# Moving the output stores of a fused RWKV and gated-SSM kernel from SyncE's queue to ScalarE's

## The chip, the cores and the metric

The kernel runs on one core of a Trainium2 chip. The metric is the device time of one execution in microseconds (us). A time is the median of several runs. A ratio is taken from the fast runs of one kernel and the fast runs of the other in the same rounds, so it is not quite the ratio of the medians quoted beside it. A run over 1.5% above the fastest of its kernel is counted as slow and left out.

Engine names in the profile: PE is TensorE, PEld its weight loads, DVE VectorE, ACT ScalarE, POOL GpSimd, SP SyncE. SPq and ACTq are the sequencers of SyncE and ScalarE, on which DMA issues and their waits stand.

## The reference

Two layers in a row. The first is a linear attention with a decaying state, for 4 x 8 heads, 768 steps and head size 48; the second is a gated state-space layer with a projection in (384 to 2 x 512), a scan, a gate and a projection out (512 to 384).

```python
for t in range(S):                                   # attention
    cur = np.einsum('bhd,bhe->bhde', u[None] * kt, vt)
    y[:, :, t] = np.einsum('bhd,bhde->bhe', rt, state + cur)
    state = wt[:, :, :, None] * state + np.einsum('bhd,bhe->bhde', kt, vt)
...
proj = x @ w_in                                      # gated state space
val, gate = proj[..., :D_inner], proj[..., D_inner:]
for t in range(S):
    h = a[0, 0] * h + val[:, t, :]
    ys[:, t, :] = h
return silu(gate) * ys @ w_out
```

The output is 4 x 768 x 384 float32, 4.72 MB, written as 24 tiles of 128 rows.

## The kernel before

The whole program is a list of words, one per step and piece. Each engine keeps the order of its own words. `ld` is a load, `osb.n` copies the result of output tile n from PSUM to SBUF on ScalarE, and `ship.n` stores it.

```python
ORDER = """
...
K.8:p xT.12 S.15 ld.9.k.0 sc.14 red.8 ...
ld.10.r.0 pv.6.1:1 S.16 scn.6.1 tr.17 K.9:p ship.4 scn.6.2 ln.11 cs.10.P:20 ship.2 sc.16 y.14
...
op.19:1 scn.11.2 op.20:0 osb.19 scn.11.3 op.21:1 ship.19 osb.20 z.11:d op.18:2 ship.20 osb.21
op.22:0 ship.21 osb.18 op.23:1 ship.18 osb.22 ship.22 osb.23 ship.23
"""
# ... cut: tiles; 7 output tiles in a ring, 3 PSUM banks for products, 1 for transposes
osbs = ring("osb", 7, [128, DM], F32)
trp = psum.tile([128, 2, HP, C], BF16, name="trp")
mms = [psum.tile([128, 512], F32, name=f"mm{i}") for i in range(3)]
# ... cut
def trd(n):                      # transpose of a q,k tile by DMA (the last six tiles)
    m, g = divmod(n, G)
    T["QK", n] = t = QKs[n % 3]
    sp.dma_start_transpose(out=..., in_=qk[m % NB][:, g]...)
# ... cut
def osb(n):
    T["osb", n] = osbs[n % 7]
    act.copy(T["osb", n], T["op", n])

def ship(n):
    b, c = divmod(n, CB)
    sp.dma_start(out=out[b, c * C : (c + 1) * C, :], in_=T["osb", n])
```

All transfers are issued by SyncE. Copies fall into three groups: six between 74 and 85 us (tiles 3, 1, 0, 4, 2, 5), twelve between 102 and 133 us, and six at the end.

## Time and profile before

| | before |
|---|---|
| median of 4 runs | 143.55 us (143.32 to 144.97) |
| span of the profiled run | 143.2 us (its device time, 144.88 us, is near the slowest of the four) |
| DMA issues | all on SyncE; 24 stores of 192 KB among them |
| ScalarE in 70 to 80 us | 9.16 of 10 us busy |

The page gives busy time, shares of 40 slices and the chain that ended last; its lines are shown in the prediction below. ScalarE's timeline before (start us, length us, engine, line, operation, output and input, count; in brackets the idle time ahead of it and what ended it):

```profile
74.72 0.85 ACT L100 COPY osb<-mm 128x384 f32<-128x384 f32 x2
75.80 0.48 ACT L100 COPY osb<-mm 128x384 f32<-128x384 f32 x1 [0.23 <-PE mm L100]
76.17 0.48 ACT L100 COPY xT<-trp 128x384 bf16<-128x384 bf16 x1
76.62 0.48 ACT L100 COPY osb<-mm 128x384 f32<-128x384 f32 x1
```

Two copies of 0.48 us take 0.85 us together, because the second starts 0.37 us after the first. ScalarE has almost no gap here.

### The profile page before, as it was taken

The numbers are of one execution on the slowest core, as the hardware profiler recorded it, in microseconds if no ns is written. First come the engines' busy times: TensorE is split into PE (matmuls) and PEld (weight loads), VectorE is DVE, ScalarE is ACT, GpSimd is POOL, SyncE is SP. The second block draws the span as 40 slices with busy tenths as digits, with TensorE's granted clock in tenths as the row PEclk, the third lists the DMA queues.
The fourth block names the chain that finished last, engine by engine and source line by source line (L and its number), as shares of the span: only waits on it lengthen the run. The fifth ranks groups of instructions, "written<-read, shape, count | busy, mean of one in ns | idle before, by whom it ended". The sixth has DMA issues, their size and how long they took to land.

```text
span 143.2 us, 3840 instructions
## 1 busy us (share of the span) xinstructions
PE 116.9 (82%) x1512; PEld 80.6 (56%) x1512; DVE 114.8 (80%) x169; ACT 98.7 (69%) x181; POOL 88.5 (62%) x83
## 2 busy tenths in 40 slices
PE   0288583899577797997799899998999999999990
PEld 0124351477354545876567677865477676767750
DVE  3026899658897679999999999889969989979740
ACT  3294636695767469999897899998587608645461
POOL 7814222195479485944949769983467999295500
PEclk9999999999999879999999999999599999999999
DMA  3999998999999899999999999898999999930435
GB/s 48 236 184 208 213 223 139 232 220 190 232 203 218 189 196 278 173 223 225 267 179 165 202 183 206 170 207 224 182 185 228 179 270 285 240 115 0 165 128 206
DMA packets 101026, 27.98 MB, mean 195 GB/s; under 512 B 95760, under 2 KB 101008, under 8 KB 101008
## 3 DMA queue, kind: packets, MB, share of 16 engines
q1 hardware_dynamic: 101008, 27.73, 95.8%
q8 instruction: 12, 0.20, 0.6%
q14 instruction: 6, 0.05, 0.1%
HBM read 21.43 MB, written 4.72 MB: 183 GB/s over the span
## 4 chain that ended last, share of the span: by engine, by line
PE 23%; SPq 22%; DMA 18%; DVE 16%; ACT 7%; issue 7%; POOL 5%; POOLq 0%; DVEq 0%; ACTq 0%
SPq L100 22%; PE mm L100 14%; DMA QK<-qk 6%; PE yk L100 5%; DVE At L100 4%; DMA stage<-in_moe_w_out_dram 4%; DMA r<-in_r_dram 4%; DMA k<-in_k_dram 3%; DVE hT L100 3%; DVE rk L100 3%; DVE y L100 3%; PE trp L100 2%; POOL dv L100 2%; POOL qk L100 2%; ACT QK L100 2%
## 5 line engine op out<-in xcount | busy, mean ns | idle before, releaser
L100 PE MATMUL mm<-xT,w_in_sb 128*128 128x256 bf16 x288 | 38.9, 279 | 0.8 <-ACT xT L100 0.6
L100 PEld LDWEIGHTS <-w_in_sb 128*128 128x128 bf16 x288 | 26.9, 99 | 6.8 <-issue 2.2
L100 DVE TENSOR_TENSOR At<-att,mask 128x1024 bf16<-128x1024 f32 x24 | 29.1, 1213 | 1.7 <-PE att L100 1.6
L100 POOL TENSOR_TENSOR qk<-r,P 128x768 bf16<-128x768 f32 x10 | 18.2, 1818 | 15.6 <-DVE dv L100 7.6
L100 POOL TENSOR_TENSOR qk<-k,N 128x768 bf16<-128x768 f32 x11 | 20.0, 1818 | 11.0 <-DVE qk L100 4.5
L100 DVE TENSOR_TENSOR_SCAN hT<-a_f,hT,mm 128x256 bf16<-128x256 f32 x32 | 22.4, 734 | 3.2 <-PE mm L100 3.2
L100 PEld LDWEIGHTS <-qk 128*48 128x48 bf16 (+1 forms) x304 | 14.3, 107 | 12.3 <-issue 6.9
L100 ACT COPY QK<-trp 128x1024 bf16<-128x1024 bf16 x18 | 18.3, 1015 | 4.0 <-PE trp L100 3.9
L100 POOL TENSOR_TENSOR rk<-r,u_b 128x768 f32<-128x768 f32 x9 | 16.3, 1815 | 5.1 <-DMA u_b<-in_u_dram 4.9
L100 PE MATMUL mm<-w_out_sb,z 128*128 128x384 bf16 x96 | 19.2, 335 | 0.0
L100 PEld LDWEIGHTS <-QK 48*128 48x128 bf16 x352 | 11.3, 101 | 12.6 <-ACT QK L100 5.9
L100 ACT COPY osb<-mm 128x384 f32<-128x384 f32 x24 | 11.4, 479 | 8.2 <-PE mm L100 7.8
L100 ACT COPY xT<-trp 128x384 bf16<-128x384 bf16 x24 | 11.5, 480 | 7.2 <-PE trp L100 7.0
L100 DVE TENSOR_TENSOR y<-yk,dv 128x384 bf16<-128x384 f32 x24 | 13.1, 547 | 4.0 <-PE yk L100 3.6
L100 ACT ACTIVATE z<-mm 128x512 bf16<-128x512 f32 x24 | 13.8, 598 | 3.2 <-PE mm L100 3.0
L100 ACT ACTIVATE N<-mm 128x384 f32<-128x384 f32 x24 | 10.9, 492 | 7.0 <-PE mm L100 7.0
L100 POOL TENSOR_TENSOR dv<-v,dvec 128x768 f32<-128x768 f32 x9 | 13.3, 1474 | 3.7 <-DVE rk L100 2.8
L100 PE MATMUL trp<-ident,qk 128*128 128x128 bf16 x144 | 13.5, 244 | 2.3 <-POOL qk L100 1.1
L100 PE MATMUL att<-QK 48*128 48x128 bf16 x192 | 11.0, 243 | 4.8 <-ACT QK L100 3.9
L100 ACT ACTIVATE lwp<-w 128x768 bf16<-128x768 f32 (+1 forms) x13 | 10.3, 797 | 6.1 <-DMA w<-in_w_dram 6.0
L100 POOL TENSOR_TENSOR z<-z,hT 128x1024 bf16<-128x1024 bf16 x5 | 10.6, 2125 | 5.6 <-DVE hT L100 3.0
L100 DVE TENSOR_TENSOR rk<-rk,k 128x768 f32<-128x768 f32 x12 | 12.4, 1031 | 0.6 <-POOL rk L100 0.3
(52 smaller groups left out, 175.7 us busy)
## 6 DMA issues: line engine op xcount, KB each, us to landing
k<-in_k_dram SPq DMA_DIRECT2D x24, 192.0 KB, 4.6
r<-in_r_dram SPq DMA_DIRECT2D x24, 192.0 KB, 4.8
v<-in_v_dram SPq DMA_DIRECT2D x24, 192.0 KB, 4.7
out_dram<-osb SPq DMA_DIRECT2D x24, 192.0 KB, 2.4
w<-in_w_dram SPq DMA_DIRECT2D x11, 384.0 KB, 5.4
stage<-in_moe_w_in_dram SPq DMA_DIRECT2D x4, 384.0 KB, 5.0
stage<-in_moe_w_out_dram SPq DMA_DIRECT2D x2, 384.0 KB, 5.7
w<-in_w_dram SPq DMA_DIRECT2D x2, 192.0 KB, 3.4
```

The source lines that it names most:

```text
L100: return lambda *args, **kwargs: self.tc.keep_in_program_order(op(*args, **kwargs))
```

## The change

The intent is that SyncE's queue carries loads alone, and each output tile leaves as soon as it is copied. The words `ship.n` go, and the store is issued on ScalarE's queue right behind the copy.

```diff
-ld.10.r.0 pv.6.1:1 S.16 scn.6.1 tr.17 K.9:p ship.4 scn.6.2 ln.11 cs.10.P:20 ship.2 sc.16 y.14
+ld.10.r.0 pv.6.1:1 S.16 scn.6.1 tr.17 K.9:p scn.6.2 ln.11 cs.10.P:20 sc.16 y.14 adv.16 ex.10.P.0
 ... (cut: the other ship words go likewise)
     def osb(n):
         T["osb", n] = osbs[n % 7]
         act.copy(T["osb", n], T["op", n])
-
-    def ship(n):
         b, c = divmod(n, CB)
-        sp.dma_start(out=out[b, c * C : (c + 1) * C, :], in_=T["osb", n])
+        act.dma_start(out=out[b, c * C : (c + 1) * C, :], in_=T["osb", n])
```

More of the change, by code (lines that the diff above doesn't have):

```diff
@@ L59 @@
 ld.9.v.1 out.15 scn.5.3 sl.5.0 pv.6.0:0 ld.10.r.1 Q.9:p ln.10 y.15 adv.15 scn.6.0 out.14
-ld.10.r.0 pv.6.1:1 S.16 scn.6.1 tr.17 K.9:p ship.4 scn.6.2 ln.11 cs.10.P:20 ship.2 sc.16 y.14
-adv.16 ex.10.P.0 ship.1 scn.6.3 ex.10.P.1 vc.9:p trd.18 At.16 tot.10:1 QK.17 cs.10.N:02 E.10
-z.4:d yT.14 ld.10.k.1 ex.10.N.0 sc.17 tot.11:1 S.17 ru.10:p ex.10.N.1 out.16 At.17 ld.11.r.0
-E.11 cs.11.N:02 xT.14 op.8:1 ex.11.N.0 y.16 ld.10.k.0 adv.18 ex.11.N.1 rk.9 yT.15 sc.18 osb.8
-op.9:0 trd.19 xT.15 z.5:d cs.11.P:21 osb.9 out.17 z.3:d ex.11.P.0 ship.3 pg.7.0:0 At.18 Q.10:p
@@ L65 @@
-ex.11.P.1 ship.0 yT.16 pv.7.0:1 sl.7.0 ld.11.r.1 y.17 op.6:2 scn.7.0 ld.10.v.1 K.10:p out.18
-red.9 sc.19 osb.6 op.7:0 xT.16 ld.10.v.0 S.19 pg.7.1:2 osb.7 At.19 dv.9:p yT.17 ld.11.k.0
-pg.6.1:0 sl.7.1 scn.7.1 xT.17 pg.6.0:2 trd.20 sl.6.1 rk.10 op.10:1 y.18 Q.11:p pv.8.0:0
-ld.11.k.1 osb.10 red.10 sl.6.0 op.11:1 trd.21 scn.8.0 adv.19 osb.11 pg.8.0:2 z.6:p S.20 vc.10:a
-scn.8.1 sc.20 ship.8 pv.7.1:1 sl.8.0 At.20 ld.11.v.1 out.19 adv.20 ship.6 pv.8.1:0 y.19 dv.10:p
-scn.7.2 ship.5 pg.8.1:2 ld.11.v.0 S.21 sc.21 scn.7.3 K.11:p yT.18 adv.21 xT.18 scn.8.2 out.20
@@ L71 @@
-ship.9 sl.8.1 yT.19 ship.10 op.13:1 At.21 xT.19 ship.7 z.7:p op.12:2 osb.13 trd.22 y.20 pv.9.0:1
-osb.12 scn.8.3 out.21 scn.9.0 ship.11 yT.20 pv.9.1:2 vc.11:a ru.11:p y.21 ship.12 pg.9.0:0
-scn.9.1 trd.23 xT.20 S.22 op.15:1 scn.9.2 sl.9.0 sc.22 rk.11 osb.15 yT.21 op.14:0 xT.21 z.8:p
-At.22 pg.9.1:1 osb.14 adv.22 ship.14 sl.9.1 pg.10.0:0 red.11 ship.15 sc.23 scn.9.3 sl.10.0
-out.22 dv.11:p pv.10.1:1 S.23 At.23 op.16:0 z.9:p pg.10.1:2 y.22 osb.16 scn.10.2 out.23 sl.10.1
-yT.22 pv.10.0:0 y.23 xT.22 scn.10.3 yT.23 op.17:2 xT.23 scn.10.0 pv.11.0:1 osb.17 scn.10.1
@@ L77 @@
-ship.17 pg.11.1:2 scn.11.0 z.10:p ship.13 pg.11.0:0 sl.11.1 scn.11.1 ship.16 pv.11.1:2 sl.11.0
-op.19:1 scn.11.2 op.20:0 osb.19 scn.11.3 op.21:1 ship.19 osb.20 z.11:d op.18:2 ship.20 osb.21
-op.22:0 ship.21 osb.18 op.23:1 ship.18 osb.22 ship.22 osb.23 ship.23
+ld.10.r.0 pv.6.1:1 S.16 scn.6.1 tr.17 K.9:p scn.6.2 ln.11 cs.10.P:20 sc.16 y.14 adv.16 ex.10.P.0
+scn.6.3 ex.10.P.1 vc.9:p trd.18 At.16 tot.10:1 QK.17 cs.10.N:02 E.10 z.4:d yT.14 ld.10.k.1
+ex.10.N.0 sc.17 tot.11:1 S.17 ru.10:p ex.10.N.1 out.16 At.17 ld.11.r.0 E.11 cs.11.N:02 xT.14
@@ new lines @@
+op.8:1 ex.11.N.0 y.16 ld.10.k.0 adv.18 ex.11.N.1 rk.9 yT.15 sc.18 osb.8 op.9:0 trd.19 xT.15
+z.5:d cs.11.P:21 osb.9 out.17 z.3:d ex.11.P.0 pg.7.0:0 At.18 Q.10:p ex.11.P.1 yT.16 pv.7.0:1
+sl.7.0 ld.11.r.1 y.17 op.6:2 scn.7.0 ld.10.v.1 K.10:p out.18 red.9 sc.19 osb.6 op.7:0 xT.16
+ld.10.v.0 S.19 pg.7.1:2 osb.7 At.19 dv.9:p yT.17 ld.11.k.0 pg.6.1:0 sl.7.1 scn.7.1 xT.17
+pg.6.0:2 trd.20 sl.6.1 rk.10 op.10:1 y.18 Q.11:p pv.8.0:0 ld.11.k.1 osb.10 red.10 sl.6.0 op.11:1
+trd.21 scn.8.0 adv.19 osb.11 pg.8.0:2 z.6:p S.20 vc.10:a scn.8.1 sc.20 pv.7.1:1 sl.8.0 At.20
@@ new lines @@
+ld.11.v.1 out.19 adv.20 pv.8.1:0 y.19 dv.10:p scn.7.2 pg.8.1:2 ld.11.v.0 S.21 sc.21 scn.7.3
+K.11:p yT.18 adv.21 xT.18 scn.8.2 out.20 sl.8.1 yT.19 op.13:1 At.21 xT.19 z.7:p op.12:2 osb.13
+trd.22 y.20 pv.9.0:1 osb.12 scn.8.3 out.21 scn.9.0 yT.20 pv.9.1:2 vc.11:a ru.11:p y.21 pg.9.0:0
+scn.9.1 trd.23 xT.20 S.22 op.15:1 scn.9.2 sl.9.0 sc.22 rk.11 osb.15 yT.21 op.14:0 xT.21 z.8:p
+At.22 pg.9.1:1 osb.14 adv.22 sl.9.1 pg.10.0:0 red.11 sc.23 scn.9.3 sl.10.0 out.22 dv.11:p
+pv.10.1:1 S.23 At.23 op.16:0 z.9:p pg.10.1:2 y.22 osb.16 scn.10.2 out.23 sl.10.1 yT.22 pv.10.0:0
@@ L80 @@
+y.23 xT.22 scn.10.3 yT.23 op.17:2 xT.23 scn.10.0 pv.11.0:1 osb.17 scn.10.1 pg.11.1:2 scn.11.0
+z.10:p pg.11.0:0 sl.11.1 scn.11.1 pv.11.1:2 sl.11.0 op.19:1 scn.11.2 op.20:0 osb.19 scn.11.3
+op.21:1 osb.20 z.11:d op.18:2 osb.21 op.22:0 osb.18 op.23:1 osb.22 osb.23
 """
@@ L514 @@
         vc=vc, rk=rk, ru=ru, red=red, dv=dv, tr=tr, trd=trd, QK=QK, sc=sc, At=At, adv=adv, S=S, out=out_,
-        y=y, yT=yT, xT=xT, pv=pv, scn=scn, pg=pg, sl=sl, z=z, op=op, osb=osb, ship=ship)
+        y=y, yT=yT, xT=xT, pv=pv, scn=scn, pg=pg, sl=sl, z=z, op=op, osb=osb)
     for word in ORDER.split():
```

## The prediction

> **What bounds the kernel now.** I read the views in this order: the busy table with the slices, the chain of waits, the queue of SyncE (its issues in time and its waits), then ScalarE's timeline around each copy that is to carry a store, and last the table by stretches. The page first, engine busy time in us, then the span in 40 slices of 3.6 us:
>
> ```profile
> PE 116.9 (82%) x1512; PEld 80.6 (56%) x1512; DVE 114.8 (80%) x169; ACT 98.7 (69%) x181; POOL 88.5 (62%) x83
> ...
> ACT  3294636695767469999897899998587608645461
> ...
> DMA  3999998999999899999999999898999999930435
> ...
> PE 23%; SPq 22%; DMA 18%; DVE 16%; ACT 7%; issue 7%; POOL 5%; POOLq 0%; DVEq 0%; ACTq 0%
> ```
>
> No engine is the bound for the whole span. The DMA engines are busy until slice 34 (about 122 us) and then have little to do; ScalarE's 69% hides a stretch, slices 18 to 28 or so, in which it is nearly full. The chain that ended last goes through SyncE's queue and transfers for 40% of the span: up to 32 us it is pure issuing of loads, from 32 to 100 us mostly computing with one transfer in it, and around 100 to 115 us a load and a transposing transfer again, from the chain in order of time (start, length, what):
>
> ```profile
> 100.90 0.43 SPq L100
> 101.33 0.06 issue
> 101.39 0.61 SPq L100
> 102.00 0.05 issue
> 102.05 4.77 DMA k<-in_k_dram
> ```
>
> A second transposing transfer, 4.91 us, stands in the chain at 122.43. After 127.4 us it is computing alone: TensorE to the last product, and a ScalarE copy at 139.60, whose store goes out at 140.1 and lands some 2 us later. What the 24 stores are today, from the list of DMA issues and SyncE's own waits:
>
> ```profile
> out_dram<-osb SPq DMA_DIRECT2D x24, 192.0 KB, 2.4
> ...
> SPq L100 <- ACT osb L100: 12.5, 7, 6.3
> ```
>
> The 12.5 us of waiting for copies are nearly all at the end, after the last load (SyncE has nothing else to do there), so they hold nothing up. The stores that stand between loads are the 13 up to 122.4 us. SyncE's issues there take 3.21 (3 stores, from 96.0), 1.05 (2), 0.52 (1), 1.09 (2), 1.64 (3) and 1.31 us (2): 8.82 us, or 0.68 us each. The first three hold data copied about 20 us before (the first six copies are at 74.7 to 84.7 us, the first store is issued at 96.0).
>
> The stretches, busy us of each engine:
>
> ```profile
> 70.00:80.00 10.00, 9.54 (x147) 6.50 (x147) 9.40 (x13) 9.16 (x20) 6.71 (x6) 1.00 0.94 173
> 80.00:90.00 10.00, 9.60 (x131) 7.43 (x131) 9.69 (x15) 8.95 (x15) 8.56 (x6) 1.00 1.17 197
> ...
> 110.00:120.00 10.00, 9.80 (x135) 6.94 (x133) 9.05 (x14) 5.22 (x11) 8.73 (x6) 1.00 1.09 224
> ```
>
> The columns are PE, PEld, DVE, ACT, POOL, then clock, DMA share and GB/s. From 70 to 90 us PE, DVE and ACT are all at 9 of 10: whatever takes time from one has little slack to hide in. From 110 on ACT has half its time free.
>
> **What the Trainium skill says.** "Perfetto Trace Analysis", section DMA Instruction — HWDGE: the semaphore wait of such an instruction sits on the issuing sequencer, and the descriptor generator is locked for it, being shared by the two sequencers that issue; the sequencer is free only when the descriptors are made. So a store on ScalarE's queue keeps ScalarE from its next instruction until the copy has ended and the issue is done. The trace of before agrees for SyncE (its issues run one after another, its waits are its own), and has no issue on ScalarE, so the lock isn't shown. "DMA: Bandwidth & Descriptors", section Issuing engines are not separate DMA queues: issues from several engines run on the same 16 DMA engines, and a second issuer saves only the sequencer's issue time. The DMA row at 9 until 122 us says that this time isn't all that SyncE is short of. "Perfetto Trace Analysis", section DMA Optimizations, speaks for the change: separating inputs and outputs between issuers may help. "ScalarE: Activation LUTs", section What ACT_TABLE_LOAD costs, has back-to-back ACTIVATEs overlapping by about 93 ns; here two output copies of 0.478 us took 0.85 us together, an overlap of about 0.11 us, which a store between them takes away.
>
> **The change part by part.** No bytes and no arithmetic change. 24 issues leave SyncE, and 24 go to ScalarE, each directly after its copy.
>
> *Taken from SyncE:* 8.82 us of issuing among the loads. The bytes stay, and the DMA engines are saturated there. In the last stretch nine stores of 192 KB run with a DMA share of about 0.46 at 161 GB/s, so a store needs about 197 KB / (161/0.46 GB/s) = 0.56 us of all engines (an estimate); 13 of them are 7.3 us, and in the changed kernel about as many have gone out before the last load. The sum doesn't fall; only its order changes: six stores move from 96 to 119 us into 75 to 86 us. What is gained is that the load at 102.05 us (4.77 us to landing, median of its kind 4.6) and the transposes (4.32 and 4.91 us) stand behind fewer bytes and reach the queue up to about a us earlier. Of 15 us of such pieces in the chain I take **2.0 us** off.
>
> *Put on ScalarE:* one store costs it the issue, about 0.35 to 0.43 us where rings are empty (shortest SyncE store 0.332, median 0.428 us), 0.68 us where loads are in flight, plus about 0.15 us for the lost overlap and for the wait until the copy's semaphore is seen (an estimate, from the 0.11 us above and the 0.02 to 0.05 us between the last copy's end and its store). So about 0.85 us in the loaded stretch, 0.5 us at the end.
>
> Stretch 74.7 to 85 us: 6 stores x 0.85 = 5.1 us. ScalarE's gaps there are 0.23 + 0.60 + 0.55 + 0.29 = 1.7 us, leaving 3.4 us. Its copies empty the single transpose bank and the three product banks, so TensorE follows; I let 80% pass: **+2.7 us**.
>
> Stretch 102 to 114 us: 6 stores, 5.1 us. ScalarE has gaps of 0.2 to 0.9 us before most of its operations, 3.8 us in sum, then a gap of 3.53 us. But each store delays the copy or activation just after it. I let a quarter pass: **+1.2 us**.
>
> Stretch 120 to 133 us: 6 stores, about 4 us, with ScalarE a third to a half free; **+0.7 us**.
>
> The end: the last six copies start at 136.23 and are 0.67 us apart on average (to 139.60), paced by products of 4 matmuls each. With 0.48 + 0.37 + 0.10 = 0.95 us for copy, issue and restart, ScalarE becomes slower than TensorE: 5 x 0.28 = **+1.4 us**. After the last copy the path (issue, 2 us of landing) is as before.
>
> Sum: 2.7 + 1.2 + 0.7 + 1.4 - 2.0 = +4.0 us, or 143.6 + 4.0 = 147.6 us.
>
> **The rivals.** *The loads run free.* If SyncE's issue time itself bounds the stretch from 96 to 123 us, where its queue has hardly a gap, taking off 8.8 us could advance the last loads and transposes by several us, and two rings per DMA engine might fill each other's gaps. For it: SPq is 22% of the chain. Against: most of that 22% is before 32 us, where there is no store; the issue times of about 1 us for loads against 0.4 us for stores say that the issuing is held by engines that are full; and PE is at 9.7 of 10 in 100 to 120 us anyway. It would give 139 to 142 us. *Everything is hidden.* ScalarE is 69% busy, with 44 us free; if the order absorbs the issues in its gaps and the delay of the middle stretch is taken back while the loads get ahead, only the end's 1.4 us remains, less the relief: 143 to 145 us. Against: the gaps of the 70 to 90 us stretch are too few. *The lock bites.* If a ScalarE issue has to wait for SyncE's running issue (load issues of about 1 us, back to back), each store of the loaded stretches costs 1.5 us or more, 12 of them 18 us instead of 10, and a good part of 8 us comes on top: 152 to 156 us. For it: SyncE's queue has no gaps from 70 to 123 us, and one store took 2.242 us to issue. Against: a store's bytes are large pieces on an otherwise empty ring.
>
> **Range and chances.** I take **147.6 us**, range **143.4 to 153.5**: the lower end is the hidden case, the upper the mild form of the lock. Faster by over 2% is below 140.7 us, only the first rival in full: 0.08. Within 2% (140.7 to 146.5) is the hidden case or a larger relief: 0.32. Slower: 0.60.
>
> **What would show it.** In the changed kernel's profile: 24 ScalarE issues of 0.35 to 0.8 us, longer in 75 to 86 us than at the end; ScalarE gaps of 0.5 to 1 us behind each output copy, put down to its own queue; TensorE and VectorE idle more for transposes and product banks from 75 us on; a ScalarE interval of about 0.95 us between the last six copies instead of 0.67; SyncE without store gaps from 96 us, and the load and transposes near 100 to 115 us landing sooner than 4.3 to 4.8 us. The prediction is wrong if the issues cost ScalarE far more (lock) or if ScalarE's delay doesn't reach TensorE; or if the chain after 96 us turns out to have been set by SyncE's queue, so that everything behind it moves up by several us.

## The result, and the profile after

The changed kernel takes 149.43 us (149.14 to 150.57, 4 runs) against 143.55 us, a ratio of 1.0403, 95% interval 1.0316 to 1.049. It is slower. Repeated later, on the same chip and in the same rounds as three of the experiments, it was 149.14 us against 145.39 us, ratio 1.0323 (1.0251 to 1.0394). Its profiled span is 147.9 us.

The page of the changed kernel, the same rows as in the prediction (busy share of ScalarE and of the DMA engines in 40 slices of 3.7 us, the chain by engine, the stores):

```profile
ACT  3284536768677579997956679998487527745541
...
DMA  3999998999989999899897999899996997711153
...
PE 36%; DVE 20%; ACT 16%; SPq 10%; issue 6%; DMA 4%; ACTq 4%; POOL 2%; DVEq 0%
...
out_dram<-osb ACTq DMA_DIRECT2D x24, 192.0 KB, 2.9
```

SyncE and DMA together fell from 40% of the chain to 14%. What replaced them is TensorE (23% to 36%) and ScalarE with its queue (7% to 20%). The span still grew by 4.7 us: the chain left the loads, and became longer.

ScalarE's timeline after, from the first output copy:

```profile
74.50 0.47 ACT L98 COPY osb<-mm 128x384 f32<-128x384 f32 x1
75.00 0.37 ACTq L98 DMA_DIRECT2D out_dram<-osb  x1
75.41 0.48 ACT L98 COPY osb<-mm 128x384 f32<-128x384 f32 x1 [0.45 <-ACT osb L98]
75.92 0.34 ACTq L98 DMA_DIRECT2D out_dram<-osb  x1
76.30 0.48 ACT L98 COPY osb<-mm 128x384 f32<-128x384 f32 x1 [0.41 <-ACT osb L98]
76.81 0.79 ACTq L98 DMA_DIRECT2D out_dram<-osb  x1
77.64 0.48 ACT L98 COPY xT<-trp 128x384 bf16<-128x384 bf16 x1 [0.86 <-PE att L98]
78.01 0.48 ACT L98 COPY osb<-mm 128x384 f32<-128x384 f32 x1
```

A store starts 0.03 us after its copy ends, holds the queue for 0.34 us, and the next operation starts about 0.05 us later. The second copy starts 0.91 us after the first instead of 0.37 us: about 0.5 us per store in which ScalarE works on nothing.

To see where the time went, I set the start of each output copy after against its start before:

| copy | 1 | 2 | 3 | 4 | 5 | 6 | 7 | 12 | 18 | 19 | 22 | 24 |
|---|---|---|---|---|---|---|---|---|---|---|---|---|
| later by, us | -0.2 | 0.3 | 0.5 | 1.4 | 2.8 | 3.0 | 3.3 | 3.6 | 2.9 | 2.9 | 4.3 | 4.8 |

So about 3 us are lost between the first and the sixth copy (74 to 88 us), nothing over the next twelve, and another 1.9 us over the last six. Such a table compares two single traces. In the repeat's trace the first copy is already 1.5 us later, with no store behind it yet, and the sixth is 3.1 us later, so only 1.6 us are lost there. Eight of the thirteen other profiles reach their first copy 0.7 to 2.3 us later than that of before, although nothing ahead of it was changed. The growth within a trace is the better guide.

The end before, and then after:

```profile
136.23 1.09 ACT L100 COPY osb<-mm 128x384 f32<-128x384 f32 x2 [1.00 <-PE mm L100]
137.65 1.08 ACT L100 COPY osb<-mm 128x384 f32<-128x384 f32 x2 [0.33 <-PE mm L100]
138.91 0.48 ACT L100 COPY osb<-mm 128x384 f32<-128x384 f32 x1 [0.17 <-PE mm L100]
139.60 0.48 ACT L100 COPY osb<-mm 128x384 f32<-128x384 f32 x1 [0.22 <-PE mm L100]
```

```profile
140.05 0.48 ACT L98 COPY osb<-mm 128x384 f32<-128x384 f32 x1 [0.47 <-PE mm L98]
140.56 0.91 ACTq L98 DMA_DIRECT2D out_dram<-osb  x1
...
143.46 0.48 ACT L98 COPY osb<-mm 128x384 f32<-128x384 f32 x1 [0.47 <-ACT osb L98]
143.96 0.34 ACTq L98 DMA_DIRECT2D out_dram<-osb  x1
144.40 0.48 ACT L98 COPY osb<-mm 128x384 f32<-128x384 f32 x1 [0.47 <-ACT osb L98]
```

Before, each of these copies waited for TensorE's product (`<-PE mm`). After, the last ones wait for ScalarE's own store, 0.94 us apart. One issue took 0.91 us, which makes this run's end 0.4 us worse than the repeat's (2.9 to 4.4 us later there).

SyncE's own waits in the changed kernel hold something that I had not foreseen (waited for: us in total, times, longest):

```profile
SPq L98 <- DMA out_dram<-osb: 7.9, 4, 4.2
```

SyncE, which now has only loads and transposes, waits for stores to land (5.7 us in 3 waits in the repeat). The compiled list of instructions says why. The compiler gives the transfers of both queues eight completion counters in turn, and a transfer waits until the one before it on its counter has landed. Two instructions of the changed kernel, one of ScalarE and one of SyncE (numbers ahead are places in each engine's order, tails of names are the compiler's; DMAHW0 to DMAHW7 are the counters):

```
98:96 L98 DMACopy out_dram<-osb_195 128x384 [waits DMAHW6_49,Activation_49]
65 L98 DMACopy r2_127<-in_r_dram 128x8x48 [waits DMAHW6_49]
```

The first is the first store; the second is a load of r with no wait but the one on the same counter. It can't go until that store has landed. The trace agrees: SyncE's issue before it ended at 75.36 us, the store was issued at 75.00 and landed at 79.58, and the load was issued at 79.59 (75.65 in the kernel before).

### The profile page after: what moved, and what is told of

It reads as the page before. It is cut to its first block, busy times and chain, and to the rows that moved or that the text cites. A ratio compares the mean times of both kernels' runs of the same rounds, so it can differ in the third digit from the quotient of the medians.

```text
span 147.9 us, 3827 instructions
## 1 busy us (share of the span) xinstructions
PE 119.0 (80%) x1512; PEld 81.4 (55%) x1512; DVE 114.0 (77%) x169; ACT 98.7 (67%) x181; POOL 88.3 (60%) x83
## 4 chain that ended last, share of the span: by engine, by line
PE 36%; DVE 20%; ACT 16%; SPq 10%; issue 6%; DMA 4%; ACTq 4%; POOL 2%; DVEq 0%
PE mm L98 21%; SPq L98 10%; PE yk L98 7%; DVE hT L98 5%; ACT osb L98 5%; PE trp L98 5%; DMA w<-in_w_dram 4%; DVE At L98 4%; ACTq L98 4%; DVE y L98 3%; ACT QK L98 3%; PE att L98 3%; DVE S L98 2%; DVE z L98 2%; DVE rk L98 2%
## 5 line engine op out<-in xcount | busy, mean ns | idle before, releaser
L98 PE MATMUL mm<-xT,w_in_sb 128*128 128x256 bf16 x288 | 39.7, 281 | 1.4 <-ACT xT L98 0.6
L98 ACT ACTIVATE P<-mm 128x384 f32<-128x384 f32 x24 | 10.8, 494 | 2.2 <-PE mm L98 1.8
```

What stands on the lines that cost most here:

```text
L98: return lambda *args, **kwargs: self.tc.keep_in_program_order(op(*args, **kwargs))
```

## The experiments

Three theories. **A:** ScalarE stands still during each store (copy wait and issue), and this costs where it is nearly full. **B:** the stores, issued early, delay loads: by their bytes (B1), or by the shared counters (B2). **C:** only the end matters. All kernels below start from the kernel before, with `ship(n, on)` able to issue on either queue (`ship.3:a` is ScalarE); all were correct.

| run | median, us | before, us | ratio (95% interval) |
|---|---|---|---|
| act_first6 | 145.92 | 144.04 | 1.0169 (1.0071 to 1.0266) |
| act_mid12 | 146.17 | 144.04 | 1.0162 (1.0057 to 1.0268) |
| act_last6 | 146.61 | 144.04 | 1.0204 (1.012 to 1.0288) |
| hold24 | 148.71 | 144.04 | 1.0337 (1.0226 to 1.0447) |
| act_lag1 | 146.49 | 144.69 | 1.0125 (1.0077 to 1.0174) |
| sp_first6_early | 145.62 | 144.69 | 1.0062 (1.0009 to 1.0115) |
| act_first6_rows16 | 146.87 | 144.69 | 1.0137 (1.0079 to 1.0194) |
| act_last18_lag1 | 146.56 | 144.69 | 1.0002 (0.9941 to 1.0064), two fast runs only |
| after_again | 149.14 | 145.39 | 1.0323 (1.0251 to 1.0394) |
| hold24_again | 148.73 | 145.39 | 1.026 (1.0207 to 1.0314) |
| hold_first6 | 145.96 | 145.39 | 1.0072 (1.004 to 1.0104) |
| act_first6_lag1 | 146.29 | 145.39 | 1.0073 (1.0041 to 1.0105) |

The medians are of all runs, the ratios of the fast ones. In the rounds of the last four rows the limit leaves out 13 of 40 runs of the kernel before, but only 4 of the 53 others. That makes these losses look somewhat larger: over all runs the means are 2.9% apart for after_again, 2.4% for hold24_again, 0.56% for hold_first6 and 0.63% for act_first6_lag1.

### Groups of stores, one at a time

act_first6:

```diff
-... osb.3 yT.9 At.13 osb.1 ld.8.r.1 ...   ship.4 ... ship.2 ... (six ship words later)
+... osb.3 ship.3:a yT.9 At.13 osb.1 ship.1:a ld.8.r.1 ...
```

> The kernel before, with only the first six stores (copies at 74 to 85 us) on ScalarE's queue directly behind their copies; the other 18 on SyncE as before. Theory A (ScalarE is held in a stretch where it is nearly full): +3.0 us, the shift of the copies between the two traces at 85 us, so about 146.5 us. Theory B (the early bytes and the waits that they put on the loads cost the time): also slower, and then the early stores on SyncE's queue must cost the same. Theory C (only the end matters): 143.5 to 144 us.

Measured 1.7% (+1.9 us), the sixth copy 2.9 us later, of which 1.6 us remain at the end. The early loss is real and is not an effect of the other stores, but smaller than the 3.0 us read from the two traces. The chain of this run shows where it lies in its profile (start us, length us, what):

```profile
74.78 0.46 ACT osb L98
75.25 0.02 issue
75.27 4.94 DMA out_dram<-osb
80.21 0.02 issue
80.22 0.37 SPq L98
...
81.54 4.30 DMA v<-in_v_dram
85.83 0.03 ACTq L98
85.86 0.04 issue
85.90 0.47 ACT vb L98
```

Here the chain doesn't run through ScalarE's standing still at all. It goes from the first copy to its store, which takes 4.94 us to land, then to SyncE, which was waiting for that landing, then to a load of v, issued late, and to ScalarE's conversion of v. That is B2. The changed kernel's own chain goes the other way over this stretch, through the copies and their stores on ScalarE, and so do those of its repeat and of act_first6_rows16 below:

```profile
74.51 0.46 ACT osb L98
...
75.00 0.37 ACTq L98
...
75.41 0.49 ACT osb L98
```

So both can be at work, and have to be parted.

act_mid12:

```diff
-... osb.8 op.9:0 ...          ship.8 ... (twelve ship words later)
+... osb.8 ship.8:a op.9:0 ...
```

> The kernel before, with only the middle twelve stores (copies at 102 to 133 us) on ScalarE's queue behind their copies. Theory A: no loss, the shift of the copies between the two traces falls by 0.4 us in this stretch, so 143.0 to 144 us. My prediction's term was +1.9 us less 2.0 us of relief, the same sum. If SyncE's queue were a bound after 96 us: 141 us or less.

A miss: 1.6% slower. Its profiled run was a slow one (147.74 us), so it can't explain what the three fast runs lost. Inside it the copies fall 3.5 us behind (from 0.3 us later at copy 9 to 3.8 us at copies 11 and 12), and the chain there has:

```profile
103.35 6.48 DMA QK<-qk
109.83 0.05 issue
109.88 0.40 PE att L97 x8
```

A transposing transfer on SyncE's queue landed 6.5 us after its issue (3.3 to 4.9 us in the six of before), and TensorE stood for it. Whether it does so in the fast runs isn't shown. In the changed kernel the same transfer landed in 3.8 us and isn't in the chain.

These stores aren't free in the changed kernel either. In four of the five kernels that change the first six stores or copies alone, 0.9 to 2.1 us of the early delay come back between copy 6 and copy 18 (act_first6: from 2.9 to 1.6 us later); in the changed kernel and in its repeat 0.1 us does. Its chain runs through copies and their stores there too (a copy at 111.05 us, its store at 111.56). SyncE also waits 3.4 us for stores to land between 107 and 113 us (1.7 us in the repeat). Which of the two keeps the delay isn't shown; holding ScalarE alone doesn't seem to, since hold24 and its repeat get 1.1 and 1.4 us back over these copies.

act_last6:

```diff
-... osb.19 scn.11.3 op.21:1 ship.19 osb.20 z.11:d op.18:2 ship.20 osb.21 ...
+... osb.19 ship.19:a scn.11.3 op.21:1 osb.20 ship.20:a z.11:d op.18:2 osb.21 ship.21:a ...
```

> The kernel before, with only the last six stores on ScalarE's queue behind their copies. Theory A: copies 0.95 us apart instead of 0.67, +1.4 to +1.9 us, 145 to 145.5 us, and together with the first six nearly all of the loss. Theory B (early bytes): no loss, 143.5 us, since nothing is loaded there.

2.0% slower. In the trace its last copies are 0.95 us apart and the shift grows from -0.4 to 1.0 us, 1.4 us; the timed loss is larger than that. C falls, since the first six lose as well. The three groups add to 5.4%, the changed kernel loses 3.2% to 4.0%: the losses aren't additive, one group's delay hides another's.

### ScalarE held, nothing stored from it

hold24 and hold24_again:

```diff
         act.copy(T["osb", n], T["op", n])
+        act.copy(T["osb", n], T["osb", n])
```

> The kernel before, all stores on SyncE as before, but each output copy is followed by a second copy of the tile onto itself (same values), which keeps ScalarE about 0.5 us longer after its first copy, as a store does, without any change to transfers. Theory A: as slow as the changed kernel, 148 to 151 us. Theory B (the order of transfers is what costs): 143.5 to 145 us.

> The run in which every output copy is done a second time and no store is moved, once more: its first look had a profiled run 1.9 us longer in span than that of before, its timed runs 3.4% more. If standing still is all of the loss, it is as slow as the changed kernel in the same rounds, 4% over before. If the shared counters make a part of 1 to 1.5 us, it is 2.5 to 3.3% over before and the changed kernel about 1% slower than it.

3.4%, and 2.6% in the repeat. All transfers keep their queue and their order, and ScalarE's standing still is replaced by work of about the same length:

```profile
74.59 0.47 ACT L97 COPY osb<-mm 128x384 f32<-128x384 f32 x1
75.10 0.51 ACT L97 COPY osb<-osb 128x384 f32<-128x384 f32 x1
75.52 0.47 ACT L97 COPY osb<-mm 128x384 f32<-128x384 f32 x1
```

Output copies are 0.93 us apart, as in the changed kernel (0.91 us). So holding ScalarE alone makes most of the loss: 2.6 of 3.2 points in the same rounds. A part of the 2.6 is the second copy's own: the last store now waits for it and goes out 0.57 us after the last product's copy ended (0.03 us in the changed kernel), about 0.5 us or 0.4 points, so some 2.2 points compare. B1 and B2 can't be the main cause. The two kernels' intervals overlap, so the rest is not shown by this pair alone.

### The store behind the next instruction

act_lag1: each store one ScalarE instruction later.

```diff
-... osb.3 ship.3:a yT.9 At.13 osb.1 ship.1:a ld.8.r.1 op.4:1 osb.0 ship.0:a xT.9 ...
+... osb.3 yT.9 At.13 osb.1 ship.3:a ld.8.r.1 op.4:1 osb.0 ship.1:a xT.9 ship.0:a ...
```

> All 24 stores on ScalarE's queue as in the changed kernel, but each one ScalarE instruction later than its copy (the very last stays behind its own), so that the wait for the copy and the issue run while ScalarE works on the next instruction. Theory A (ScalarE stands still during copy wait and issue): the last six copies are again about 0.67 us apart, and most of the loss goes, 143.5 to 145 us. Theory B (early bytes, and loads on SyncE that wait for stores to land because both queues share completion counters): the loss up to 90 us stays at 2 to 3 us, only the end's 1.4 to 1.9 us is won back, 146 to 148 us.

1.25% slower instead of 3.2% to 4.0%. The end of its trace:

```profile
138.66 0.48 ACT L98 COPY osb<-mm 128x384 f32<-128x384 f32 x1 [0.17 <-PE mm L98]
138.72 0.34 ACTq L98 DMA_DIRECT2D out_dram<-osb  x1
139.38 0.48 ACT L98 COPY osb<-mm 128x384 f32<-128x384 f32 x1 [0.25 <-PE mm L98]
139.44 0.73 ACTq L98 DMA_DIRECT2D out_dram<-osb  x1
```

The issue now runs while ScalarE copies the next tile. The copies wait for TensorE again and are 0.66 us apart from 138.01 to 141.33 us, as before (0.67 us): the end's loss is gone. At the start SyncE still waits 4.0 us for a store, and the second store's issue took 1.59 us, with ScalarE idle for 1.21 us. This fits A for the larger part of the loss; the rest can be B2, or that one long issue.

### The early bytes and the shared counters

sp_first6_early:

```diff
-... osb.3 yT.9 At.13 osb.1 ld.8.r.1 ...   ship.4 ... ship.2 ... (six ship words later)
+... osb.3 ship.3 yT.9 At.13 osb.1 ship.1 ld.8.r.1 ...        (SyncE's queue)
```

> The kernel before, with the first six stores on SyncE's queue at once behind their copies (SyncE waits for each copy in its order), nothing on ScalarE. Theory A: ScalarE isn't touched, at most 1 us of loss from SyncE's waiting, 143.5 to 145 us. Theory B: the loads behind them are as late as in the run of the first six on ScalarE, +1.5 to +2.5 us, 145.5 to 146.5 us.

0.6% slower, inside A's expectation. The same bytes leave nearly as early, 75.8 us for the first. This run is no clean test of the bytes: SyncE's loads stand behind the stores and their copies here, and go later too (numbers below).

act_first6_rows16:

```diff
-... osb.3 ship.3:a yT.9 ...
+... osb.3 ship.3:t yT.9 ...   ship.4:r ... (t: rows 0 to 15 on ScalarE; r: the other 112 on SyncE)
+        lo, hi = {"t": (0, 16), "r": (16, C)}.get(on, (0, C))
```

> The kernel before, with 16 of the 128 rows of each of the first six tiles stored from ScalarE behind the copy and the other 112 rows from SyncE where the whole store stood. ScalarE's issues and the shared counters are as in the run of the first six on ScalarE, the early bytes are an eighth. Theory A or shared counters: 145.5 to 146.5 us as there. If it is the early bytes that delay the loads: 144 to 145 us, and the first store lands well before the 4.9 us that it took there.

1.4% slower, little less than with whole tiles (1.7%), although the first 24 KB store landed in 2.8 us instead of 4.9. SyncE's longest wait for a store is still 4.4 us. B1, the early bytes, isn't needed to explain the loss; the two intervals are too wide to say that it has no share.

hold_first6 and act_first6_lag1 were to part the rest. The first has A without B, the second was meant to have B2 (and the early bytes) without A:

```diff
+        if n < 6:                                  # hold_first6
+            act.copy(T["osb", n], T["osb", n])
```

```diff
-... osb.3 yT.9 At.13 osb.1 ld.8.r.1 ...           # act_first6_lag1
+... osb.3 yT.9 At.13 osb.1 ship.3:a ld.8.r.1 ...
```

> The kernel before with the second copy for the first six output tiles alone. Holding ScalarE alone: the shift at the sixth copy was 1.4 us in the run with all 24 held and fell to 0.5 us later, so 0.3 to 1.0% slower. If the whole early loss is holding: 1.7% as with the first six stores on ScalarE.

> The first six stores on ScalarE one instruction after their copies, the others on SyncE as before: no standing still, but the same shared counters and the same early bytes. If the counters hold the loads: SyncE waits some 4 us for the first store to land, and 0.7 to 1.2% slower. If holding ScalarE is all: within 0.5% of the kernel before.

0.72% and 0.73%, with narrow intervals; together they make 1.45%, near the 1.69% of act_first6. The first is A alone. The second isn't B2 alone: ScalarE is held once after all, by a long issue, as in act_lag1.

```profile
77.13 0.48 ACT L98 COPY osb<-mm 128x384 f32<-128x384 f32 x1 [0.22 <-PE mm L98]
77.19 1.41 ACTq L98 DMA_DIRECT2D out_dram<-osb  x1
78.63 0.48 ACT L98 COPY xT<-trp 128x384 bf16<-128x384 bf16 x1 [1.03 <-PE att L98]
```

0.98 us of this issue stand in the chain, and over it the copies fall back by 1.2 us (from 1.3 us later at the third to 2.5 at the fourth). What made the issue long isn't shown. SyncE's waits have this line:

```profile
SPq L98 <- DMA out_dram<-osb: 3.3, 1, 3.3
```

The pair of v loads that follows is issued 4.5 us after the first output copy there, 6.0 us in the changed kernel and 6.3 in act_first6, but 3.4 us in the kernel before and 3.2 in hold_first6. So with stores on ScalarE these loads go 1 to 3 us later; that the counters are why rests on the compiled waits and on these issue times. What it costs isn't shown: of these traces only act_first6's chain goes through the late pair, and in act_first6_lag1 the 0.73% can as well be the long issue. In sp_first6_early the pair is late too (4.9 us), by SyncE's own order, stands in the chain, and 0.6% is lost. A kernel in which only the counters differ could not be made, since the compiler assigns them. So of the early loss 0.7% is shown to be standing still; the rest is shared between longer issues, late loads and early bytes in parts that stay open.

### The changed kernel again

The edit is none; it was run for the ratio.

> The changed kernel once more, on the same chip and in the same rounds as the three below, so that their losses can be set against its own. 3% to 5% slower than the kernel before; its last six copies 0.95 us apart.

3.2%; its last six copies are 0.97 us apart on average.

### A version without both

act_last18_lag1: the first six stores on SyncE as before, the others as in act_lag1.

> The first six stores on SyncE where they were, the other 18 on ScalarE one instruction after their copies. This takes both suspected losses away. Theory A and B alike: 143 to 144.5 us, within 1% of the kernel before; below 142.5 us only if freeing SyncE's queue after 100 us is worth something. If it is over 145 us, a third cause (transposes on SyncE that land late beside stores from the other queue, as in the run of the middle twelve) is at work.

Inconclusive. Two of four runs were fast (145.3 and 144.32 us) and equal to the kernel before; the two others, 148.29 and 147.83 us, were over the limit for a slow run. The profiled run is one of the slow ones, and in it what the expectation called a third cause stands, from the chain:

```profile
113.14 6.93 DMA QK<-qk
120.06 0.05 issue
120.11 0.40 PE att L98 x8
```

As in act_mid12, a transposing transfer lands very late beside stores from the other queue. A transpose landed in 5.5 us also in act_first6 and in 5.6 us in act_last6, with no ScalarE store near. Since the two latest landings are of slow runs, whether the stores cause them, and whether they cost anything in fast runs, stays open. No version here beats the kernel before, so none is put forward.

## Why the prediction was right, and where its steps were off

The prediction said slower, 147.6 us in a range of 143.4 to 153.5; 149.43 us was measured. The direction and the main cause, ScalarE held where it is nearly full and at the end, hold. The predicted loss was 4.0 us and the timed one 5.9 us; the 1.9 us that are missing are about the relief of 2.0 us, which never came; that the other terms add up so well is partly luck. Its terms:

- **The cost of one store.** "0.68 us where loads are in flight, plus about 0.15 us": too large. ScalarE's issues have a median of 0.338 us, with 0.79 us at most among loads in the changed kernel, and the whole hold is 0.5 us. SyncE's longer issues (a median of 0.99 us for its loads from 70 to 123 us in the kernel before) were met on the second queue only singly (0.79 and 0.91 us here, 1.59 us in act_lag1).
- **74.7 to 85 us, "+2.7 us".** The first trace shows 3.0 us by the sixth copy, the repeat's only 1.6 us, and the agreement is partly luck. With 0.5 us a store, the same working gives 6 x 0.5 - 1.7 = 1.3 us, x 0.8 = 1.0 us, and hold_first6 measured 0.72% of 145 us, 1.0 us. act_first6 lost 1.69%; the rest of it is not parted into longer issues (0.79 us here, 1.41 in act_first6_lag1), late loads and early bytes. The tie by shared counters is something that the prediction hadn't.
- **102 to 133 us, "+1.2 us" and "+0.7 us".** The changed kernel is 3.3 us later at copy 7 and 2.9 us at copy 18. Since kernels without these stores on ScalarE get 0.9 to 2.1 us back here, the stores cost about that, of the order of the predicted 1.9 us, but holding ScalarE isn't shown to be why (hold24 gets its time back). Alone they lost 1.6%, with the cause open.
- **The end, "+1.4 us".** 0.95 us per copy was predicted, and 0.94 us between most copies was measured; the loss is 1.4 us in act_last6's trace, 1.5 us in the repeat's and 1.9 us in the first, with its one issue of 0.91 us.
- **Relief for SyncE, "2.0 us off".** This is the step that failed. From 98 us on no load or transpose is left in the chain, but at most 0.4 us came back (from copy 7 to 18). The transposes landed in 3.8 to 5.3 us, no sooner than before. TensorE was 9.8 to 10.0 of 10 us busy from 110 to 130 us, and SyncE spent 7.9 us in waits for stores. The rival in which the loads run free is refuted with it.
- **The lock.** Refuted at the size feared: nine of the 24 ScalarE issues overlap one of SyncE's, and none of the nine took over 0.37 us. From the queues' timelines of the changed kernel:

```profile
85.44 1.12 SPq L98 DMA_DIRECT2D r<-in_r_dram  x1
```

```profile
85.53 0.36 ACTq L98 DMA_DIRECT2D out_dram<-osb  x1
```

- **Small slips.** The 8.82 us counts the short gaps between stores; the 13 issues alone are 8.35 us, 0.64 us each. The chain has two transfers between 32 and 100 us, not one (loads at 32.02 and 65.13 us). A quarter of 5.1 us is 1.3 us. None changes the forecast.

One thing more stays open. In the changed kernel's profile TensorE's clock is low for some us in the very stretch of the early loss (columns: window, length, busy PE, PEld, DVE, ACT, POOL, then granted clock, DMA share, GB/s):

```profile
78.50:80.50 2.00, 1.78 (x29) 1.37 (x29) 1.17 (x2) 1.53 (x4) 0.70 (x1) 0.71 0.61 217
80.50:82.50 2.00, 2.00 (x19) 0.88 (x17) 0.00 (x0) 0.92 (x3) 0.80 (x2) 0.50 0.83 167
```

Six matmuls there took 1.44 us instead of 0.82. Such dips are in every profile of these runs, at places that differ from run to run: slices from 48, 78 and 104 us here, from 41, 70 and 103 us in the repeat, from 47 and 100 us in that of before. They can make part of a shift between two traces, this one part of the 3.0 us, which is why the shares of the loss are taken from the timed runs. What sets them off was not tested.

## What to carry to other kernels

A DMA issue on a computing engine costs that engine the wait for its own last result plus the issue, 0.5 us here, so put it behind the next instruction of that engine rather than behind the one whose result it ships: this alone took the loss from between 3.2% and 4.0% down to 1.25%. Before a queue is split in two, look at what the transfers of both share: counters that tie a load to a store of another engine can stop the loads until that store has landed (4.2 us here), though what that cost in time was not parted from the rest. And an engine's average busy share (69%) says little: holding it cost time where it was at 92%, and at the end, where its pace took over from TensorE's.

## What the Trainium skill lacked or had wrong

- "Perfetto Trace Analysis", section DMA Instruction — HWDGE, has the issuing sequencer wait for the semaphore and then lock the shared descriptor generator. The wait on the sequencer agrees (a store starts 0.03 us after its copy ends, and the next operation after the store). A lock held through an issue isn't seen: nine ScalarE issues overlap one of SyncE's and take 0.34 to 0.37 us, one of them, of 0.36 us, within a SyncE issue of 1.12 us.
- The same page, section DMA Optimizations, says that separating inputs and outputs between issuers may help, above all with loops or control flow, which this program hasn't. Here it cost 3.2% to 4.0%, and the section doesn't say what it costs a computing engine: 0.34 us of issue, 0.5 us with the wait for the copy and the restart, nearly nothing if another instruction runs meanwhile (0.66 us between copies at the end instead of 0.95), though single issues took up to 1.59 us.
- "DMA: Bandwidth & Descriptors", section Issuing engines are not separate DMA queues: that a second issuer only saves issue time agrees; no gain came from it in any of these runs. No page that I read says that two queues can be tied by completion counters which the compiler deals out to both, 7.9 us of waits on SyncE here.
- None of the pages read has how long a DMA transpose takes beside other transfers: 3.3 to 4.9 us from issue to landing in the kernel before, up to 5.3 us in the changed kernel, and 6.5 and 6.9 us in two slow runs with ScalarE stores near it.
